# Score and value products that stream 32 copies of their one moving column, in a cached-attention decode kernel

## The chip, the cores and the metric

The kernel runs on one core of one Trainium2 chip. Its time is the device time in microseconds (us) of that core, the median of several runs. "Clock" is the share of its full clock that the throttle grants to TensorE; it is either 0.5 or 1.0 at any moment, so a mean is a share of time. In the trace of the kernel before it stays at one of them for whole multiples of 3.41 us (27 stretches, the last left out); a *window* is one such step of 3.41 us. A program on one core was fast in nearly all runs; the few slow are left out of ratios. The chip differed between the calls of the study, so runs are compared by way of the kernel before, which ran beside each of them.

## The reference, cut to what matters

One token, 32 heads, 32,768 cached keys of 128 numbers each, all bf16. K and V together are 537 MB, and each is read once.

```python
x = A_x
q = (_layernorm(x) @ wq)                        # 32 heads of 128
scores = einsum("bhqd,bhkd->bhqk", q, k_cache) * Dh ** -0.5
p = softmax(scores)
o = einsum("bhqk,bhkd->bhqd", p, v_cache)
h = x + o.reshape(1, 1, 4096) @ wo
h2 = h + B(_layernorm(h))                       # 512 -> 1376 -> 512, mish
```

## The kernel before

Keys lie on partitions. A *block* is 128 keys; a *group* is 8 blocks of one head (1,024 groups in all, 32 a head). For each group the PE transposes 8 blocks of K into PSUM, the DVE copies them to SBUF, and the PE multiplies each transposed block by the one column of q. Values lag by 42 groups: each block of V is multiplied by the one column of probabilities that belongs to it. K and V arrive through a ring of 160 KB a partition, in loads of 32 KB a partition (4.19 MB, 16 groups of K or of V). A load may start only when the PE has used up what lay in its place.

```python
def transposes(i):                   # group i
    ...
    for r in range(R):               # R = 8
        S.step(PE, lambda r=r: t_.matmul(
            tb[:, r * 128:(r + 1) * 128], block(ld, i, r), identb[:, :],
            is_transpose=True, start=True, stop=True), ...)

def scores(i):
    ...
    for r in range(R):
        c = (i % GH) * R + r
        S.step(PE, lambda r=r, c=c: t_.matmul(
            Sb[:, c:c + 1], kt[:, i % NE, r * 128:(r + 1) * 128], qT[:, h:h + 1], start=True, stop=True), ...)

def values(i):
    ...
    for r in range(R):
        c = (i % GH) * R + r
        S.step(PE, lambda r=r, c=c: t_.matmul(
            ob[:, 0:1], block(ld, i, r), pbuf[:, h % 2, c:c + 1],
            start=(c == 0), stop=(c == NCOL - 1)), ...)

for i in range(END):                 # order on the PE: transposes(i), scores(i - 2), values(i - 42)
    ...
    if 0 <= ho < H - 1 and (i - LAG) % GH == 3:
        y_cols(ho)                   # output projection of a finished head, as columns
    if i == NK + LAG + 8:            # near the end, once:
        for h in range(H - 1):
            y_mean(h)                # 62 matmuls
        for h in range(H - 1):
            y_row(h)                 # 124 matmuls, the same projection as rows
# after the loop: last head, layer norm, feed-forward, output
```

Of the kernel before, what the change touches and what calls it, by code (L numbers as in the profile page):

```python
# [19 lines left out]
RING_BYTES = 160 * 1024  # L20
LAG = 10
NSEM = 24


class _Sched:
# [89 lines left out]
def plan_loads(H, GH, ring_bytes, D, F):  # L115
# [26 lines left out]
    for i, ld in enumerate(loads):  # L142
# [11 lines left out]
        live = keep + [ld]  # L154
        if i >= NSEM:
            assert loads[i - NSEM].free is not None
            ld.after.append(loads[i - NSEM].free)
    return loads


def build_kernel(nc, A_x, A_k_cache, A_v_cache, A_wq, A_wo, B_w1, B_b1, B_w2, out, NE=3):
# [21 lines left out]
    def sb(shape, dt, name):  # L183
        cm = nc.sbuf_tensor(name, shape, dt)
        t = cm.__enter__()
        allocs.append(cm)
        return t.ap()
# [9 lines left out]
    kt = sb([128, NE, R * 128], BF16, "kt")  # L197
    pbuf = sb([128, 2, NCOL], BF16, "pbuf")
# [12 lines left out]
    qT = sb([128, 32], BF16, "qT")  # L211
# [40 lines left out]
    def view(ld):  # L252
        return ring[:, ld.off // 2:(ld.off + ld.nbytes) // 2]
# [6 lines left out]
    def block(ld, g, r):  # L260

        c = (g % GH) * R + r - ld.base
        return ring[:, ld.off // 2 + c * 128:ld.off // 2 + (c + 1) * 128]

    sem = nc.alloc_semaphore
    eng_sems = {PE: sem("ev_pe"), ACT: sem("ev_act"), DVE: sem("ev_dve"), POOL: sem("ev_pool"), SP: sem("ev_sp")}
    rsem = [sem(f"rsem{i}") for i in range(NSEM)]
    s_x = sem("s_x")
# [7 lines left out]
    def landed(ld):  # L276
        return (rsem[ld.idx % NSEM], 16 * (ld.idx // NSEM + 1))

    def program(S):
# [7 lines left out]
        def issue(ld):  # L287
            s = rsem[ld.idx % NSEM]
            dst = view(ld)
            if ld.kind in "kv":  # L290
                cache = A_k_cache if ld.kind == "k" else A_v_cache
                src = cache[0, ld.h, ld.base * 128:(ld.base + ld.n) * 128, :].rearrange("(m n) d -> m (n d)", m=128)
                S.dma(SP, lambda: sp.dma_start(dst, src).then_inc(s, 16), waits=ld.after)  # L293
            elif ld.kind == "wqa":
                S.dma(SP, lambda: sp.dma_start(
                    wqa, A_wq[:, 0:NH0 * Dh].rearrange("(p kc) n -> p kc n", kc=KC)).then_inc(s, 16), waits=ld.after)
            elif ld.kind == "wqb":
                S.dma(SP, lambda: sp.dma_start(
                    wqb, A_wq[:, NH0 * Dh:HD].rearrange("(p kc) n -> p kc n", kc=KC)).then_inc(s, 16), waits=ld.after)
            elif ld.kind == "w1":  # L300
                S.dma(SP, lambda: sp.dma_start(
                    w1v, B_w1.rearrange("(kc p) f -> p kc f", p=128)).then_inc(s, 16), waits=ld.after)
            else:
                S.dma(SP, lambda: sp.dma_start(
                    w2v[:, 0:FJ - 1, :],
                    B_w2[0:(FJ - 1) * 128, :].rearrange("(j p) n -> p j n", p=128)).then_inc(s, 16), waits=ld.after)
                S.dma(SP, lambda: sp.dma_start(
                    w2v[0:FLAST, FJ - 1, :], B_w2[(FJ - 1) * 128:F, :]).then_inc(s_w2, 16))
# [75 lines left out]
        def scores(i):  # L384
            h = i // GH
            Sb = S_b[h % 2]
            waits = [f"ev{i}", "qT0" if h < NH0 else "qT"]
            if i % GH == 0 and h >= 2:
                waits.append(f"exp{h - 2}")
            for r in range(R):  # L390
                c = (i % GH) * R + r
                S.step(PE, lambda r=r, c=c: t_.matmul(  # L392
                    Sb[:, c:c + 1], kt[:, i % NE, r * 128:(r + 1) * 128], qT[:, h:h + 1], start=True, stop=True),
                    name=(f"qkb{i}" if r == R - 1 else None), waits=(waits if r == 0 else ()))

        def values(i):
            h = i // GH
            ld = vload[i]
            ob = o_b[h % 2]
            waits = []  # L400
            if i % GH == 0:
                waits.append(f"exp{h}")
                if h >= 2:
                    waits.append(f"oT{h - 2}")
            if (i % GH) * R == ld.base:
                waits.append(landed(ld))
            for r in range(R):
                c = (i % GH) * R + r
                S.step(PE, lambda r=r, c=c: t_.matmul(  # L409
                    ob[:, 0:1], block(ld, i, r), pbuf[:, h % 2, c:c + 1],  # L410
                    start=(c == 0), stop=(c == NCOL - 1)),
                    name=(f"pv{i}" if r == R - 1 else None), waits=(waits if r == 0 else ()))

# [40 lines left out]
        for i in range(END):  # L454
# [11 lines left out]
            if 0 <= i - 2 < NK:  # L466
                scores(i - 2)
# [30 lines left out]
            if i - GH - LAG >= 0:  # L498
                values(i - GH - LAG)
# [41 lines left out]
        for j in range(FJ):  # L541
            W = 128 if j < FJ - 1 else FLAST
            for kc in range(KC):
                S.step(PE, lambda j=j, W=W, kc=kc: t_.matmul(  # L544
                    pre[0:W, j:j + 1], w1v[:, kc, j * 128:j * 128 + W], xcT[:, kc:kc + 1],
                    start=(kc == 0), stop=(kc == KC - 1)),
# [18 lines left out]
        for j in range(FJ):  # L565
            W = 128 if j < FJ - 1 else FLAST
            waits = ["act", landed(by_kind["w2"]), (s_w2, 16)] if j == 0 else ()
            for c in range(KC):
                S.step(PE, lambda j=j, W=W, c=c: t_.matmul(  # L569
                    yps[32 * c:32 * c + 1, HROW:HROW + 128], actT[0:W, j:j + 1], w2v[0:W, j, c * 128:(c + 1) * 128],  # L570
                    start=False, stop=(j == FJ - 1), skip_group_check=True),
# [47 lines left out]
```

## Time and profile before

| | before |
|---|---|
| time, median of 3 runs | 1389.87 us (1383.92 to 1392.62) |
| profiled span | 1381.0 us |
| PE busy | 96% |
| mean clock | 0.559 |
| DMA queue 1 (all loads), share of 16 engines | 95.0% |

These are lines of the page of the kernel before. Part 1 gives busy us, the share of the span and the count of instructions; part 2 cuts the span into 40 slices and gives tenths; part 3 gives packets, MB and share of the engines' time; part 4 is the chain of waits that ended last; part 5 gives busy us and mean ns of a group of instructions, then the idle time before it.

```profile
span 1381.0 us, 52251 instructions
PE 1326.2 (96%) x25319; PEld 1306.5 (95%) x25319; DVE 762.3 (55%) x1245; ACT 20.5 (1%) x70; POOL 2.5 (0%) x10
...
PE   6859999999999999999999999999999999999997
...
PEclk9856555555555565775565555555555555565556
DMA  9999999999999999999999999999999999999994
...
DMA packets 28298, 551.44 MB, mean 399 GB/s; under 512 B 2648, under 2 KB 8632, under 8 KB 11192
...
q1 hardware_dynamic: 27992, 548.09, 95.0%
q8 instruction: 198, 3.24, 0.9%
...
PE 94%; DMA 4%; issue 2%; SPq 0%; DVE 0%; ACT 0%
...
L373 PE MATMUL tps<-identb,ring 128*128 128x128 bf16 x8192 | 984.0, 296 | 19.5 <-DMA ring<-in_A_k_cache_dram 9.0
```

PE and DMA are both full, so the shares do not tell which one paces. The waits of the DMA's own queue (this view has: who waited for whom, us in total, times, the longest):

```profile
SPq L293 <- PE ops L409: 837.9, 61, 28.7
SPq L293 <- PE sps L392: 448.4, 61, 22.5
```

The queue waits for the PE to free the ring. The PE waits for loads only some 20 us in all:

```profile
PE ops L409 <- DMA ring<-in_A_v_cache_dram: 11.2, 1, 11.2
PE tps L373 <- DMA ring<-in_A_k_cache_dram: 9.0, 3, 4.8
```

The PE paces. The timeline (start, length, instruction) of the kernel before shows that it has two speeds, first at clock 0.5, then at clock 1.0:

```profile
660.64 1.01 PE L373 MATMUL tps<-identb,ring 128*128 128x128 bf16 x8
661.45 0.40 PE L392 MATMUL sps<-qT,kt 128*128 128x1 bf16 x8
661.71 0.35 PE L409 MATMUL ops<-pbuf,ring 128*128 128x1 bf16 x8
661.92 1.01 PE L373 MATMUL tps<-identb,ring 128*128 128x128 bf16 x8
...
700.72 0.61 PE L373 MATMUL tps<-identb,ring 128*128 128x128 bf16 x8
701.16 0.34 PE L392 MATMUL sps<-qT,kt 128*128 128x1 bf16 x8
701.37 0.34 PE L409 MATMUL ops<-pbuf,ring 128*128 128x1 bf16 x8
701.57 0.61 PE L373 MATMUL tps<-identb,ring 128*128 128x128 bf16 x8
```

Read starts, not lengths, for matmuls overlap. From transposes to the next transposes a group takes 1.28 us at half clock (660.64 to 661.92) and 0.85 us at full clock (700.72 to 701.57). K and V of a group need about 1.23 us of DMA: loads of 16 groups, of K or of V, land every 9.7 to 9.9 us in this trace when nothing holds them up. So the PE is a little slower than the DMA at half clock and far faster at full clock, and it runs at half clock most of the time.

### The profile page before, as it was taken

What the parts mean: (1) busy time and instruction counts of PE and PEld (TensorE: products, weight loads), DVE (VectorE), ACT (ScalarE), POOL (GpSimd) and SP (SyncE); (2) the same over time, 40 slices, a digit from 0 to 9 for tenths busy, and PEclk for the clock granted to TensorE, in tenths of its full rate; (3) what the DMA queues carried; (4) which work ended last, traced back from release to release, by engine and by line L of the source; (5) the groups of instructions that cost most, each with busy time, mean ns of one, the idle gap of its engine ahead of it and who ended that gap; (6) DMA issues with size and microseconds to landing.
All of it is one profiled execution on the core that took longest, in us unless ns stands there. A gap on an engine that the chain in (4) does not pass through costs nothing.

```text
span 1381.0 us, 52251 instructions
## 1 busy us (share of the span) xinstructions
PE 1326.2 (96%) x25319; PEld 1306.5 (95%) x25319; DVE 762.3 (55%) x1245; ACT 20.5 (1%) x70; POOL 2.5 (0%) x10
## 2 busy tenths in 40 slices
PE   6859999999999999999999999999999999999997
PEld 6859999999999999999999999999999999999997
DVE  5626555555555555665565555555555555555562
ACT  0000000000000000000000000000000000000000
POOL 0000000000000000000000000000000000000000
PEclk9856555555555565775565555555555555565556
DMA  9999999999999999999999999999999999999994
GB/s 390 402 422 419 433 425 430 428 396 414 402 385 417 390 396 411 420 421 421 419 410 417 409 387 397 403 391 404 395 391 407 392 393 396 385 428 387 389 391 156
DMA packets 28298, 551.44 MB, mean 399 GB/s; under 512 B 2648, under 2 KB 8632, under 8 KB 11192
## 3 DMA queue, kind: packets, MB, share of 16 engines
q1 hardware_dynamic: 27992, 548.09, 95.0%
q8 instruction: 198, 3.24, 0.9%
q14 instruction: 12, 0.10, 0.0%
q0 software_dynamic: 96, 0.00, 0.0%
HBM read 548.08 MB, written 0.00 MB: 397 GB/s over the span
## 4 chain that ended last, share of the span: by engine, by line
PE 94%; DMA 4%; issue 2%; SPq 0%; DVE 0%; ACT 0%
PE tps L373 60%; PE ops L409 16%; PE sps L392 14%; DMA ring<-in_A_k_cache_dram 4%; PE hlp L480 1%; PE hlp L485 1%; PE hlp L494 1%; SPq L293 0%; PE yps L431 0%; PE yps L417 0%; PE hlp L358 0%; PE yps L424 0%; PE sps L544 0%; PE yps L569 0%; DVE kt L382 0%
## 5 line engine op out<-in xcount | busy, mean ns | idle before, releaser
L382 DVE COPY kt<-tps 128x1024 bf16<-128x1024 bf16 x1024 | 707.2, 691 | 581.8 <-PE tps L373 580.7
L373 PE MATMUL tps<-identb,ring 128*128 128x128 bf16 x8192 | 984.0, 296 | 19.5 <-DMA ring<-in_A_k_cache_dram 9.0
L373 PEld LDWEIGHTS tps<-identb,ring 128*128 128x128 bf16 x8192 | 746.2, 134 | 23.7 <-issue 10.9
L392 PEld LDWEIGHTS sps<-qT,kt 128*128 128x128 bf16 x8192 | 412.2, 113 | 9.7 <-issue 9.5
L392 PE MATMUL sps<-qT,kt 128*128 128x1 bf16 x8192 | 401.1, 170 | 8.9 <-issue 8.8
L409 PE MATMUL ops<-pbuf,ring 128*128 128x1 bf16 x8192 | 355.6, 165 | 13.9 <-DMA ring<-in_A_v_cache_dram 11.2
L409 PEld LDWEIGHTS ops<-pbuf,ring 128*128 128x128 bf16 x8192 | 298.5, 104 | 26.4 <-issue 14.6
L489 ACT ACTIVATE pbuf<-sps,nbias 128x256 bf16<-128x256 f32 x32 | 15.1, 473 | 1334.4 <-DVE nbias L487 1334.4
L447 DVE TENSOR_REDUCE wbar<-wo_sb 128x1 f32<-128x512 bf16 x32 | 21.6, 674 | 0.0
L494 PE MATMUL hlp<-esum,onesm 128*128 128x1 f32 x64 | 17.9, 346 | 0.9 <-issue 0.9
L480 PE MATMUL hlp<-ident,pmax 128*1 128x128 f32 x64 | 18.4, 387 | 0.1
L485 PE MATMUL hlp<-gmax,onesr 1*128 1x1 f32 x64 | 18.1, 350 | 0.0
L494 PEld LDWEIGHTS hlp<-esum,onesm 128*128 128x128 f32 x64 | 15.8, 303 | 1.0 <-issue 1.0
L485 PEld LDWEIGHTS hlp<-gmax,onesr 1*128 1x128 f32 x64 | 15.4, 296 | 0.5
L476 DVE TENSOR_REDUCE pmax<-sps 128x1 f32<-128x256 f32 x32 | 13.3, 416 | 2.0 <-PE sps L392 2.0
L482 DVE TENSOR_REDUCE gmax<-hlp 1x1 f32<-1x128 f32 x32 | 8.9, 279 | 1.2 <-PE hlp L480 0.7
L417 PE MATMUL yps<-oT,wo_sb 128*128 128x1 bf16 x128 | 7.8, 165 | 0.3 <-DVE oT L530 0.3
L496 DVE RECIPROCAL rtotc<-hlp 128x1 f32<-128x1 f32 x32 | 5.4, 168 | 2.4 <-PE hlp L494 2.4
L358 PE MATMUL hlp<-xnT,ring 128*128 128x1 bf16 x128 | 3.8, 164 | 3.0 <-issue 3.0
L358 PEld LDWEIGHTS hlp<-xnT,ring 128*128 128x128 bf16 x128 | 3.6, 99 | 3.2 <-issue 3.1
L502 DVE TENSOR_SCALAR oT<-ops,rtotc 128x1 bf16<-128x1 f32 x31 | 6.6, 211 | 0.0
L530 DVE TENSOR_SCALAR oT<-ops,rtotc 128x1 bf16<-128x1 f32 x1 | 0.2, 221 | 11.2 <-PE ops L409 11.2
(69 smaller groups left out, 51.5 us busy)
## 6 DMA issues: line engine op xcount, KB each, us to landing
ring<-in_A_k_cache_dram SPq DMA_DIRECT2D x62, 4096.0 KB, 14.6
ring<-in_A_v_cache_dram SPq DMA_DIRECT2D x62, 4096.0 KB, 16.9
ring<-in_A_k_cache_dram SPq DMA_DIRECT2D x2, 2048.0 KB, 10.7
ring<-in_A_v_cache_dram SPq DMA_DIRECT2D x2, 2048.0 KB, 18.3
wo_sb<-in_A_wo_dram SPq DMA_DIRECT2D x1, 4096.0 KB, 37.7
ring<-in_A_wq_dram SPq DMA_DIRECT2D x1, 3584.0 KB, 30.2
ring<-in_A_k_cache_dram SPq DMA_DIRECT2D x2, 1024.0 KB, 9.6
ring<-in_A_v_cache_dram SPq DMA_DIRECT2D x2, 1024.0 KB, 22.4
```

The costliest lines, as they stand in the source:

```text
L373: S.step(PE, lambda r=r: t_.matmul(tb[:, r * 128:(r + 1) * 128], block(ld, i, r), identb[:, :], is_transpose=True, start=True, stop=True), ...
L382: S.step(DVE, lambda: v.tensor_copy(kt[:, i % NE, :], T_b[i % 2][:, :]), name=f"ev{i}", waits=waits)
L392: S.step(PE, lambda r=r, c=c: t_.matmul(Sb[:, c:c + 1], kt[:, i % NE, r * 128:(r + 1) * 128], qT[:, h:h + 1], start=True, stop=True), name ...
L409: S.step(PE, lambda r=r, c=c: t_.matmul(ob[:, 0:1], block(ld, i, r), pbuf[:, h % 2, c:c + 1], start=(c == 0), stop=(c == NCOL - 1)), name= ...
L417: S.step(PE, lambda c=c: t_.matmul(yps[:, c:c + 1], wo_sb[:, h, c * 128:(c + 1) * 128], oT[:, h:h + 1], start=False, stop=(h == H - 1), sk ...
L447: S.step(DVE, lambda: v.tensor_reduce(wbar[:, h:h + 1], wo_sb[:, h, :], AXX, ALU.add), waits=[(s_wo, 16)], name=f"wbar{h}")
L476: S.step(DVE, lambda hp=hp: v.tensor_reduce(pmax[:, hp:hp + 1], S_b[hp % 2][:, 0:NCOL], AXX, ALU.max), name=f"pmax{hp}", waits=[f"qkb{hp * ...
L480: S.step(PE, lambda hp=hp: t_.matmul(A_REG, pmax[:, hp:hp + 1], ident[:, :], start=True, stop=True), name=f"A{hp}", waits=[f"pmax{hp}", "i ...
L482: S.step(DVE, lambda hp=hp: v.tensor_reduce(gmax[0:1, hp:hp + 1], A_REG, AXX, ALU.max), name=f"gmax{hp}", waits=[f"A{hp}"])
L485: S.step(PE, lambda hp=hp: t_.matmul(B_REG, onesr[0:1, :], gmax[0:1, hp:hp + 1], start=True, stop=True), name=f"B{hp}", waits=[f"gmax{hp}" ...
L489: S.step(ACT, lambda hp=hp: a.activation(pbuf[:, hp % 2, :], S_b[hp % 2][:, 0:NCOL], ACTF.Exp, bias=nb[:, hp:hp + 1], scale=SC, accum_out= ...
L494: S.step(PE, lambda hp=hp: t_.matmul(C_REG, onesm[:, :], esum[:, hp:hp + 1], start=True, stop=True), name=f"C{hp}", waits=[f"exp{hp}"])
```

## The change

The intent: each product with a one-column moving operand streams 32 copies of it, so that the array is seen to be busier and the throttle grants the full clock. The extra result columns are overwritten or never read. There are no more instructions than before, and their order is the same.

```diff
+WIDE = 32
@@ scores
-                    Sb[:, c:c + 1], kt[:, i % NE, r * 128:(r + 1) * 128], qT[:, h:h + 1], start=True, stop=True),
+                    Sb[:, c:c + WIDE], kt[:, i % NE, r * 128:(r + 1) * 128], qT[:, h:h + 1].to_broadcast([128, WIDE]),
+                    start=True, stop=True),
@@ values
-                    ob[:, 0:1], block(ld, i, r), pbuf[:, h % 2, c:c + 1],
+                    ob[:, 0:WIDE], block(ld, i, r), pbuf[:, h % 2, c:c + 1].to_broadcast([128, WIDE]),
                     start=(c == 0), stop=(c == NCOL - 1)),
```

## The prediction

> **What bounds it now.** The page shows PE busy 96% of a 1381 us span, DMA queue 1 busy 95%, mean granted clock 0.559. The chain of waits is 94% PE, 4% DMA. The queue's own waits are nearly all for PE lines (838 + 448 us): loads wait until PE frees ring space. PE paces the kernel, the DMA close behind.
>
> Per group of 8 blocks (1024 groups) the timeline shows two speeds: 1.28 us at clock 0.5 (transposes 107 ns start to start, scores and values 27 ns), 0.85 us at clock 1.0 (55 and 25 ns). A full-size load (4.19 MB) lands every 9.7 to 9.9 us when not held up (87 to 247 us), about 426 GB/s, so K and V of a group need 1.23 us.
>
> **Why the clock is low.** Granted stretches last multiples of 3.41 us[...]. In the slow steady state the array streams 8x128 + 16 = 1040 columns in 1.28 us, 68%[...]. The clock rises only after windows in which most transposes fall (22 to 24, about 75%), and falls after starved ones. I infer that streamed columns are counted, transposes included, with a threshold near 75%.[...]
>
> **The change** removes nothing, moves no instruction, and adds 31 streamed columns to each of 16,384 products. Cost at half clock: 32 columns are 26.7 ns by estimate (128 take 107), within the 27 ns[...]. At full clock 14 ns, under the 25 ns spacing. So about +0. Benefit: activity at half clock goes to 1536 columns[...], so every busy half-clock window should lift the clock.
>
> **Then DMA binds.** PE needs at most about 16 us for 16 groups, even with two half-clock windows (6.8 us, 5.3 groups, the rest at 0.85), against 19.8 us of DMA. PE will starve some us every 16 groups and the clock will drop then: mixed, but off the critical path. Estimate: 128 full loads x 9.9 = 1268 us, output weights 13, other weights about 16, start 2.5: DMA ends near 1300. PE, now 14 us behind when the last V lands (1358 to 1372), should be under 1 us behind. The last V lands 3.5 us before the last weights; from the last value product to the end stays 8.6 us. Span 1306 to 1310, plus 2 us outside it.
>
> **Predicted: 1312 us, 8 in 10 within 1296 to 1340. Faster by over 2%: 0.92; within 2%: 0.05; slower: 0.03.**
>
> **What would show it.** Mean clock 0.7 to 0.85; products still 27 and 25 ns apart; a chain mostly DMA; queue 1 busy 98% or more, about 420 GB/s; PE waits on K and V loads of 200 us or more; PE busy near 75%.
>
> **What would make it wrong.** If 32 columns don't overlap the weight load (54 ns, or slow reads of a repeated element), half clock costs 1.7 us a group: possibly slower. If the clock counts something else, it stays near 0.55 and nothing changes. If DMA can't hold 426 GB/s while PE runs fast, 1330 to 1345. Long clock drops shrink the gain.

128 full loads 1268 us, output weights 13, other weights 16 and the start 2.5 make 1299.5, the "near 1300" of the text. All four are from the trace before: 13 is what the landing of the output weights adds to one interval between loads (22.9 us in place of 9.7), 16 is an estimate (7.0 MB at 426 GB/s), 2.5 us is when the first input lands. The 68% is a share of the 1536 columns that transposes one after the other, 128 columns every 106.7 ns on average in that trace, would stream in 1.28 us. The estimates of 26.7 and 14 ns for 32 columns are a quarter of the 107 and 55 ns of a transpose, and 54 ns is 27 measured plus 26.7 estimated; that wider products would cost nothing was not shown before the result.

## The result, and the profile after

| | before | after |
|---|---|---|
| time, median of the fast runs of this comparison (4 each) | 1388.09 us | 1332.03 us |
| ratio, 95% interval | | 0.9595 (0.9558 to 0.9632) |
| profiled span | 1381.0 us | 1331.3 us |
| PE busy | 96% | 77% |
| mean clock | 0.559 | 0.889 |
| last V lands / last value product done | 1358.1 / 1372.4 us | 1314.4 / 1322.6 us |

A ratio is the mean time of one kernel's fast runs over that of the other's of the same rounds, so it is not quite the ratio of the medians. The change is faster by 4%. The lines of the page after that answer to those above:

```profile
span 1331.3 us, 52251 instructions
PE 1031.1 (77%) x25319; PEld 999.0 (75%) x25319; DVE 753.8 (57%) x1245; ACT 20.5 (2%) x70; POOL 2.5 (0%) x10
...
PE   6838778777788778877778778778778777777776
...
PEclk9879888889888898898899889899888898898885
DMA  9999999999999999999999999999999999999993
...
DMA packets 28298, 551.44 MB, mean 414 GB/s; under 512 B 2648, under 2 KB 8632, under 8 KB 11192
...
q1 hardware_dynamic: 27992, 548.09, 97.4%
q8 instruction: 198, 3.24, 1.0%
...
DMA 66%; PE 31%; issue 2%; SPq 0%; DVE 0%; ACT 0%
...
L375 PE MATMUL tps<-identb,ring 128*128 128x128 bf16 x8192 | 701.6, 234 | 171.7 <-DMA ring<-in_A_k_cache_dram 133.5
```

The chain has turned from PE to DMA, and the PE has gaps in every slice. Instruction for instruction nothing got slower: products start 27 to 28 ns apart at half clock and 25 ns at full clock, as before. The waits of the PE in the kernel after:

```profile
PE tps L375 <- DMA ring<-in_A_k_cache_dram: 133.5, 58, 5.6
PE sps L394 <- issue: 48.0, 35, 2.3
PE ops L412 <- issue: 46.5, 36, 2.4
PE tps L375 <- issue: 35.7, 33, 2.3
PE ops L412 <- DMA ring<-in_A_v_cache_dram: 16.5, 3, 15.0
```

Two kinds of idle time share the gaps: 150 us for loads and 130 us of "issue", in which nothing that the profile shows is waited for. The second kind comes 104 times, 1.25 us on average, and is new in this size (20 us in the kernel before). It is a wait for instructions. Queue q8 brings them in packets of 16 KB, one every 6.5 us or so, and all 96 "issue" waits of the PE over 0.5 us end 1.2 to 1.6 us after such a packet has ended. In the kernel before the same holds for all 16 of them.

Landing times, read from the loads' semaphores, give the pace of the DMA. Over 110 loads in the middle of the trace a load lands every 10.02 us on average after, against 10.37 us before. But the pace is not even: most intervals are 9.7 us, and 21 of the 110 are about 11.3 us, one in five or six. Finally the tail of the kernel after, from its timeline (brackets: idle time of the engine before it):

```profile
1307.72 1.26 PE L427 MATMUL yps<-oT,wbh 128*128 128x1 bf16 x42
1310.95 0.69 PE L427 MATMUL yps<-oT,wbh 128*128 128x1 bf16 x20 [1.97 <-issue]
1311.57 3.05 PE L434 MATMUL yps<-wo_sb,oT 128*1 128x128 bf16 x108
1317.16 0.59 PE L434 MATMUL yps<-wo_sb,oT 128*1 128x128 bf16 x16 [2.54 <-issue]
1317.68 4.94 PE L412 MATMUL ops<-pbuf,ring 128*128 128x32 bf16 x184
1322.66 0.22 DVE L533 TENSOR_SCALAR oT<-ops,rtotc 128x1 bf16<-128x1 f32 x1 [15.54 <-PE ops L412]
```

The last V lands at 1314.4 us. The PE is then still in the block of means and rows, in which it waits twice for instructions; 184 value products come after it.

### The profile page after: what moved, and what is told of

Its sections match the earlier page's. It is cut to its first block, busy times and chain, and to the rows that moved or that the text cites. A ratio compares the mean times of both kernels' runs of the same rounds, so it can differ in the third digit from the quotient of the medians.

```text
span 1331.3 us, 52251 instructions
## 1 busy us (share of the span) xinstructions
PE 1031.1 (77%) x25319; PEld 999.0 (75%) x25319; DVE 753.8 (57%) x1245; ACT 20.5 (2%) x70; POOL 2.5 (0%) x10
## 4 chain that ended last, share of the span: by engine, by line
DMA 66%; PE 31%; issue 2%; SPq 0%; DVE 0%; ACT 0%
DMA ring<-in_A_k_cache_dram 64%; PE tps L375 16%; PE ops L412 7%; PE sps L394 6%; DMA ring<-in_A_v_cache_dram 2%; PE hlp L483 1%; PE hlp L488 1%; PE hlp L497 1%; PE yps L434 0%; SPq L295 0%; PE yps L427 0%; PE sps L547 0%; PE yps L572 0%; SPq L297 0%; PE yps L420 0%
## 5 line engine op out<-in xcount | busy, mean ns | idle before, releaser
L375 PE MATMUL tps<-identb,ring 128*128 128x128 bf16 x8192 | 701.6, 234 | 171.7 <-DMA ring<-in_A_k_cache_dram 133.5
L375 PEld LDWEIGHTS tps<-identb,ring 128*128 128x128 bf16 x8192 | 523.6, 104 | 183.2 <-DMA ring<-in_A_k_cache_dram 137.3
L394 PE MATMUL sps<-qT,kt 128*128 128x32 bf16 x8192 | 382.6, 180 | 48.2 <-issue 48.0
L412 PE MATMUL ops<-pbuf,ring 128*128 128x32 bf16 x8192 | 366.1, 179 | 63.1 <-issue 46.5
L394 PEld LDWEIGHTS sps<-qT,kt 128*128 128x128 bf16 x8192 | 334.6, 100 | 51.2 <-issue 51.1
L412 PEld LDWEIGHTS ops<-pbuf,ring 128*128 128x128 bf16 x8192 | 283.9, 98 | 77.0 <-issue 59.6
L497 PE MATMUL hlp<-esum,onesm 128*128 128x1 f32 x64 | 12.0, 253 | 1.0 <-issue 0.9
L488 PE MATMUL hlp<-gmax,onesr 1*128 1x1 f32 x64 | 12.3, 259 | 0.0
L497 PEld LDWEIGHTS hlp<-esum,onesm 128*128 128x128 f32 x64 | 9.8, 192 | 1.0 <-issue 1.0
L492 ACT ACTIVATION_READ_ACCUMULATOR pbuf<-sps,nbias 128x1 f32 x32 | 6.2, 193 | 0.0
```

Of the source, the lines that this page charges most:

```text
L375: S.step(PE, lambda r=r: t_.matmul(tb[:, r * 128:(r + 1) * 128], block(ld, i, r), identb[:, :], is_transpose=True, start=True, stop=True), ...
L394: S.step(PE, lambda r=r, c=c: t_.matmul(Sb[:, c:c + WIDE], kt[:, i % NE, r * 128:(r + 1) * 128], qT[:, h:h + 1].to_broadcast([128, WIDE]), ...
L412: S.step(PE, lambda r=r, c=c: t_.matmul(ob[:, 0:WIDE], block(ld, i, r), pbuf[:, h % 2, c:c + 1].to_broadcast([128, WIDE]), start=(c == 0), ...
L488: S.step(PE, lambda hp=hp: t_.matmul(B_REG, onesr[0:1, :], gmax[0:1, hp:hp + 1], start=True, stop=True), name=f"B{hp}", waits=[f"gmax{hp}" ...
L492: S.step(ACT, lambda hp=hp: a.activation(pbuf[:, hp % 2, :], S_b[hp % 2][:, 0:NCOL], ACTF.Exp, bias=nb[:, hp:hp + 1], scale=SC, accum_out= ...
L497: S.step(PE, lambda hp=hp: t_.matmul(C_REG, onesm[:, :], esum[:, hp:hp + 1], start=True, stop=True), name=f"C{hp}", waits=[f"exp{hp}"])
```

## The experiments

Theory: the throttle counts streamed columns, transposes among them; the change lifts that count over a threshold, the PE is no longer the pace, and the DMA binds. Rivals: transposes do not count; the gain grows with the columns themselves; the PE still co-limits through its stalls. A second question came with the result: where do the 11.3 us intervals come from?

A caution for all that follows. The comparison with the reference passed even for a run that leaves out seven of eight products of most heads. Attention adds too little to this output for that comparison to see it. So "correct" says little about attention here, for any kernel in this document.

### The phase run: what the clock counts

Edit: the whole program is replaced by PE phases over one loaded block of K, with an idle stretch before each (wrong result). The core of it:

```diff
+PHASES = [("N", 1), ("T", 0), ("N", 8), ("M", 1), ("N", 16), ("M", 4), ("N", 20),
+          ("M", 8), ("N", 24), ("M", 16), ("N", 28), ("M", 32), ("N", 32)]
+# T: transposes; N: products with n columns; M: 8 transposes, 16 products with n columns
+# before each phase the PE waits for two large memsets on the DVE
```

> A kernel of PE phases alone (wrong result on purpose, no ring, no loads but one of 256 KB): each phase of some 50 us at half clock is preceded by an idle stretch on PE, so each starts at half clock. Phases in order: products with 1 column; transposes; products with 8 columns; the group mix (8 transposes, 16 products) with 1 column; products 16; mix 4; products 20; mix 8; products 24; mix 16; products 28; mix 32; products 32. My theory (the clock counts streamed columns, transposes included, with a threshold near 75%): clock stays 0.5 in products 1, 8, 16, 20 (3 to 62%[...]); rises within two windows (6.8 us) in transposes (100%), products 28 and 32, mix 16 and 32 (83%, 100%); products 24 and mix 1, 4, 8 (75%, 68, 71, 75%) lie near the threshold: mix 1 late or not at all, mix 8 soon. Rival (transposes do not count, only ordinary products do): the transposes phase stays at 0.5 to its end, and mix 16 or 32 (17%, 33%) rises only if products 8 (25%) rises too.

Measured, with each phase's activity (columns streamed, as a share of those that transposes one after the other stream in the same time at half clock, 128 every 107 ns), and when the clock rose after the phase's start:

| phase | activity | clock rose after | then |
|---|---|---|---|
| products, 1 / 8 / 16 / 20 columns | 3 / 25 / 49 / 62% | never in 50 us | |
| mix, 1 column (the kernel before) | 68% | never in 51 us | |
| mix, 4 columns | 71% | 11.2 us | stayed |
| mix, 8 columns | 75% | 7.4 us | stayed |
| products, 24 columns | 74% | 4.6 us | fell again after 10.2 us |
| mix, 16 columns | 83% | 4.9 us | stayed |
| products, 28 columns | 86% | 6.4 us | fell once after 24 us, back 3.4 us later |
| mix, 32 / products, 32 columns | 100 / 99% | 2.6 / 5.0 us | stayed |
| transposes alone | 100% | 4.6 us | stayed |

Lines of the view by windows of that run (columns: window, its length and the PE's busy us; then busy us of the other engines, granted clock, DMA share, GB/s), for the mix with 1 column, the mix with 4, and the transposes:

```profile
270.80:322.00 51.20, 51.20 (x960) 51.20 (x960) 0.00 (x0) 0.00 (x0) 0.50 0.01 3
442.50:480.20 37.70, 37.70 (x958) 37.70 (x959) 0.00 (x0) 0.00 (x0) 0.85 0.01 3
121.40:150.30 28.90, 28.90 (x479) 28.90 (x480) 0.00 (x0) 0.00 (x0) 1.00 0.01 2
```

PE busy is 100% in all three, so it is not busy time that is counted. Columns fit: with the transposes counted in full, the mix stayed at half clock at a mean of 68% and rose at 71%, so the threshold of this run lies between the two. The rival falls. The kernel before sits just under it, which is why its clock rose only now and then. My guess of 75% was for single windows of 3.41 us, and is not settled: those that ended in a rise hold 75% or more here and 71% or more in the kernel before, but other windows of up to 76% brought no rise.

The way down is another count. At full clock transposes start 55 to 56 ns apart in place of 107, so shares are here taken of twice as many columns. In this run every window that ended in a fall held at most 36% of them, and every one that did not, 39% or more; in the kernel before these figures are 35 and 36%, and in the other traces the two kinds overlap between 34 and 39%. Products with 24 columns stayed up through two windows at 40%; they fell, and those with 28 too, in a window with a gap of 0.5 or 0.8 us in which the PE waited for instructions.

### Few bytes, one column and 32: the PE without the DMA

Edit, on top of either kernel (wrong result). A first try of both, cut from head 2 on and to one eighth, was REFUSED before the chip, because a part of the ring was read unwritten; it gave no result. This is the second:

```diff
+                if ld.h >= 4:
+                    cut = ld.nbytes // 16
+                    dst, src = dst[:, 0:cut], src[:, 0:cut]
```

> The refused one-column kernel again, with the K and V loads of heads 4 to 31 cut to one sixteenth (wrong result on purpose; the ring is written in full before, so nothing is read unwritten). PE alone sets the pace from head 4 on. If starved windows were what kept the kernel before at half clock: the clock rises early and stays, mean above 0.85, span about 1020 to 1090 us. If 68% activity is too little by itself (the phase run left the same mix at half clock for its whole 51 us): clock stays near 0.5 with few stretches of 1.0 at per-head work, span 1300 to 1380 us. In that kernel no starved window ends a stretch of 1.0, so such stretches should be long.

> The same cut (heads 4 to 31, one sixteenth of the bytes) in the changed kernel, 32 columns. PE is the only limit at 0.85 us a group: about 150 us for the first four heads at the pace of DMA, 900 groups x 0.85 = 765, extras 40 and the tail: 960 to 1030 us, mean clock above 0.95. Instruction stalls of PE should nearly vanish[...]: under 40 us against 130 us in the changed kernel. Rival (PE co-limits the changed kernel): over 1200 us.

Measured, one run each: one column 1072.86 us, clock 0.834; 32 columns 1002.85 us, clock 0.968, with instruction waits on the PE of about 19 us in place of 130. With most of the DMA's work gone the changed kernel runs in 1003 us. The cut removes most of the PE's instruction waits too, but with their 130 us added it would still be far under 1332. So the DMA, not the PE, holds it there, and that rival falls.

The one-column run is the more instructive. Its clock fell to 0.5 at 76 us, stayed there for 307 us (the first 90 or so still under full loads), rose at 383 us and then stayed at 1.0 for 662 us, to the tail. So two things held the kernel before at half clock. At 68% it seldom crosses the threshold (I had said early; it took 307 us). And each rise is short, but not for want of loads: in the kernel before, the PE waits for its last load at 97 us. Each of its nine falls between 100 and 1360 us ends a window of 3.41 us in which the PE waited 0.4 to 1.9 us for instructions. This wait comes before the fall at 708.6 us:

```profile
707.26 0.25 PE L392 MATMUL sps<-qT,kt 128*128 128x1 bf16 x4 [1.61 <-issue]
```

At full clock the PE uses its instructions up 1.5 times as fast (0.85 us a group in place of 1.28), and under full loads their packets then come too late. In the few-bytes run such waits add up to 6 us. Once up and fed, one column is enough: 1040 columns in 0.85 us are 51% by the count at full clock.

### Widths 4 and 8

Edit: `WIDE = 4`, and `WIDE = 8`.

> WIDE = 4 in place of 32: activity at half clock 70.8% (1088 of 1536). The phase run lifted the clock of this mix after 11 us and kept it. Theory of a threshold near 70%: after each starved stretch about 11 us at half clock (8.7 groups), then fast: 16 groups in about 17.4 us, still under the DMA's 19.9, so mean clock 0.65 to 0.85 and 1332 to 1352 us. If per-head work and phase leave it under the threshold: clock under 0.6 and over 1370 us, as before. If the gain grew with the columns themselves (31 extra give 56 us, 3 give a tenth): about 1380 us.

> WIDE = 8: activity 75% at half clock. The phase run lifted the clock of this mix after 7.4 us. Threshold theory: at most three half-clock windows after a starved stretch, 16 groups in about 16.5 us, DMA paces: clock 0.75 to 0.88, 1331 to 1341 us. If the gain were proportional to the extra columns (7 of 31 of 56 us): about 1375 us.

| WIDE | mean clock (profiled run) | median | ratio to before of the same rounds |
|---|---|---|---|
| 4 | 0.638 | 1351.88 us (1337.67 to 1357.28) | 0.9713 (0.9616 to 0.981) |
| 8 | 0.784 | 1332.59 us (1331.57 to 1334.71) | 0.9591 (0.9562 to 0.962) |
| 32 | 0.889 | 1332.03 us | 0.9595 (0.9558 to 0.9632) |

Eight columns give all of the gain, at a lower mean clock, and four give some 70% of it by the mean ratios, though the interval for four is wide (2 to 4% faster). It is a threshold, not a proportion, by which four would have given a tenth. Above it, more clock buys nothing (1332.59 us at 0.784, 1332.03 at 0.889), because the DMA binds. The 4-column run varied by 20 us, and its clock (just under my range) and time lie at the edge. Of its 30 falls between 70 and 1300 us, 29 come with an instruction wait, and after a fall it can rise late (the longest stretch at half clock is 154 us).

### Products cut: the DMA's floor, and the periodic step

Edit, on the changed kernel (wrong result), for transposes, scores and values alike; the start flag of the values follows:

```diff
-            for r in range(R):
+            for r in (range(R) if i < 2 * GH else [R - 1]):
```

> The changed kernel with all its loads, but from head 2 on only one transpose, score and value product of each eight (wrong result on purpose): the DMA floor, and about 7 of 8 PE instructions gone, so few instruction blocks to fetch. Theory A (the periodic extra 1.5 us in every fifth to sixth load, 11.3 against 9.7 us, is PE's instruction blocks taking DMA time): loads land every 9.7 us nearly throughout, last V about 30 us earlier, span 1285 to 1302 us. Theory B (the periodic step belongs to the loads or the memory): the step stays at one in five or six loads, span 1318 to 1330 us. Either way at most 8 us of the changed kernel's tail goes with PE's backlog.

Measured: 1294.65 us (4 runs within 0.4 us), ratio 0.9351. Intervals are 9.7 us nearly throughout: only 4 of 110 exceed 10.5 us. Its instruction queue:

```profile
q8 instruction: 40, 0.66, 0.2%
```

There are 40 packets of 16 KB against 198. The last V lands at 1284.1 us, 30.3 us earlier than in the changed kernel, and 8.9 us later all is done, against 16.9. This is what theory A said, but the run also took away the PE's reads of the ring, so it does not tell A from B alone.

### Instructions put back without their work

Edit, on the run with products cut: where an instruction was dropped, a 1 x 1 matmul stands in its place.

```diff
+                if r < R - 1 and i >= 2 * GH:
+                    S.step(PE, lambda: t_.matmul(
+                        Sb[0:1, 400:401], oneb[0:1, 0:1], oneb[0:1, 0:1], start=True, stop=True), ...)
+                    continue
```

> The run with products cut (1294.65 us), but each of the seven transposes, scores and values taken out of eight is replaced by a 1 x 1 matmul with its own weight load: the instruction count is that of the changed kernel again, the array's work and its reads of the ring stay small. Theory A (instruction blocks cost the DMA about 0.19 us each): the step of 1.5 us in every fifth to sixth load is back, instruction queue near 198 packets, last V near 1314 us, span 1322 to 1334 us. Theory B (it was PE's reads of the ring, or its fast work, that disturbed the loads): loads stay at 9.7 us, span 1290 to 1300 us.

> As the run with 1 x 1 matmuls in place, but only the cut scores and values are replaced, the cut transposes are left out: PE[...] should no longer pace anything, and the instruction blocks are two thirds of the way back (about 145 packets against 40 and 198). Theory A (0.19 us of DMA per block, from 30.3 us over 158 blocks): last V at 1284 + 105 x 0.19 = 1304 us, 1311 to 1322 us in all. Theory B (PE's reads of the ring and fast work disturb the loads): last V at 1284 to 1288 us, under 1303 us in all.

The first of them, with all three kinds put back, was a poor experiment. It took 1347.94 us: small as they are, these matmuls cost the PE so much that a group took 1.2 us, the PE was 97% busy and paced again. The longer intervals were back and the last V landed at 1316.7 us, but with two limits so close it proves little.

The second, with scores and values alone put back, left the PE 74% busy at half clock:

| run | instruction packets | last V lands | intervals over 10.5 us, of 110 |
|---|---|---|---|
| products cut | 40 | 1284.1 us | 4 |
| two thirds put back | 145 | 1302.1 us | 15 |
| the changed kernel | 198 | 1314.4 us | 21 |

It took 1319.25 us, with the last V within 2 us of theory A's figure and 14 us beyond theory B's range, though these matmuls read nothing of the ring and the clock was 0.526. So the step is the PE's instruction stream on the DMA engines: 30.3 us over 158 packets is 0.19 us each, and by that estimate about 38 us of the changed kernel's time. In the trace of the changed kernel a 16 KB instruction packet takes 0.9 to 1.1 us, and nine in ten of them overlap with exactly one 32 KB load packet that takes about 1.7 us in place of 1.22. How the longer packet becomes the longer interval is not shown.

### The tail moved into the loop

Edit, on the changed kernel. The sums of the output weights are also spread over the first part of the loop, so that the means have them in time.

```diff
                 y_cols(ho)
+                y_row(ho)
...
-            if i == NK + LAG + 8:
-                for h in range(H - 1):
-                    y_mean(h)
-                for h in range(H - 1):
-                    y_row(h)
+            if i > WB + 4 and ym_next < H - 1 and (ym_next < ho or (ym_next == ho and (i - LAG) % GH > 3)):
+                y_mean(ym_next)
+                ym_next += 1
```

> The changed kernel itself, on the chip of this call, so that the next two can be compared with it: 1328 to 1335 us.

> The changed kernel with the output rows and means of heads 0 to 30 moved out of the tail: the rows right after the head's output columns, the means one a step from the middle on (the sums of the output weights are taken earlier for it). Nothing added, nothing removed. In the changed kernel 10 us of the last 22 lie in that block (5.5 us of matmuls, 4.5 us waiting for instructions), and the last V lands 8 us before PE reaches it. Expected: PE finishes within 1 us of the last V, 5 to 8 us saved, about 1324 us, and the last V lands where it did. Rival (the waits for instructions move to other places of the tail, or the second weights land last): under 3 us saved.

Measured in the same rounds, 6 runs each: the changed kernel 1331.60 us (ratio 0.9604), this one 1324.62 us (0.9551; 1323.94 to 1325.64). The 7.0 us are inside what was expected. The last V lands at 1313.6 us as it did (1313.5), and the PE finishes 1.6 us later, in place of 8.2 in the first profile of the changed kernel and 5.5 in that of these rounds; I had said within 1 us.

### Packed value products

Edit, on the last one: p is the stationary operand and four blocks of V the moving one; the four diagonal blocks of the result are added once a head.

```diff
+                for r in range(0, R, 4):
+                    c = (i % GH) * R + r
+                    o = ld.off // 2 + (c - ld.base) * 128
+                    S.step(PE, lambda r=r, c=c, o=o: t_.matmul(
+                        ob[0:4, 0:512], pbuf[:, h % 2, c:c + 4], ring[:, o:o + 512],
+                        start=(c == 0), stop=(c == NCOL - 4)), ...)
```

> The last one, and value products packed: four columns of the weights are the stationary operand and four blocks of V (512 columns) the moving one, two matmuls a group in place of eight; the diagonal 128-column blocks of the 4 x 512 result are added by four small matmuls a head (last head as before). PE instructions fall by a quarter, from 198 blocks to about 150. Theory A: 48 x 0.19 = 9 us of DMA back, 1311 to 1319 us; clock above 0.9, since half of the array's time more is streaming. PE needs about 1.07 us a group, so its margin to the DMA (1.23) is thin: if instruction stalls of 0.1 us a group come on top, PE paces again and it takes 1320 to 1345 us.

It failed: 1379.56 us (ratio 0.9943), with clock 0.986 and 152 packets. Both figures were as hoped, but the PE paced, at 1.27 us a group (the 1.07 was an estimate: 8 transposes at 55 ns, 8 scores at 25 and 1024 columns of V at 55 for 128):

```profile
700.56 0.09 PEld L416 LDWEIGHTS ops<-ring,pbuf 128*4 128x4 bf16 x2
700.56 0.59 PE L416 MATMUL ops<-ring,pbuf 128*4 128x512 bf16 x2
701.08 0.45 PEld L377 LDWEIGHTS tps<-identb,ring 128*128 128x128 bf16 x8 [0.44 <-issue]
701.09 0.62 PE L377 MATMUL tps<-identb,ring 128*128 128x128 bf16 x8
```

The two matmuls need 0.43 us (215 ns each, as measured in the next run), but the next transposes start 0.53 us after the first of them, and their weight load does not start before. In all, 107 ns pass before the packed matmuls in place of 25, and 311 ns after the second in place of 215. The weight load does not run beside the streaming here: PEld is idle for 0.44 us before it. The next edit asks whether the narrow stationary operand is the reason:

```diff
-                        ob[0:4, 0:512], pbuf[:, h % 2, c:c + 4], ring[:, o:o + 512],
+                        ob[:, 0:512], pbuf[:, h % 2, c:c + 128], ring[:, o:o + 512],
```

(p is padded with zeros; rows from 4 on of the result are not used.)

> The packed value products once more. In the last run PE needed 1.27 us a group at full clock in place of 1.07: after the matmuls with a 4-column stationary operand the next transposes started 311 ns later in place of 215, and before them 107 ns passed in place of 25. Here the stationary operand is 128 columns of the weights (only the first four rows of the result are used), so that it loads like every other and its load can hide. Expected: those gaps at 215 and 25 ns, PE 1.07 us a group, no pacing by PE, 152 blocks, last V near 1306 us, 1312 to 1322 us in all against 1324.6 with the tail moved alone. Rival (the drain belongs to the 512-column matmul itself): 1.27 us a group again, about 1380 us. Between: instruction stalls make PE pace, 1322 to 1345 us.

Measured: 1314.80 us (1314.41 to 1315.21), ratio 0.9462 (0.944 to 0.9484). The same place of its timeline:

```profile
701.32 0.12 PEld L418 LDWEIGHTS ops<-ring,pbuf 128*128 128x128 bf16 x2
701.35 0.59 PE L418 MATMUL ops<-ring,pbuf 128*128 128x512 bf16 x2
701.56 0.65 PEld L378 LDWEIGHTS tps<-identb,ring 128*128 128x128 bf16 x8
701.77 0.61 PE L378 MATMUL tps<-identb,ring 128*128 128x128 bf16 x8
```

The load of the transposes' weights now starts 0.21 us before them, the gaps are 215 and 25 ns, and a group takes 1.08 us. The last V lands at 1303.5 us, 10 us earlier than with 198 packets, which repeats the cost of an instruction packet (10 us over 46 packets, 0.22 us each) in a kernel that does its full work. This version beats both kernels: 1.4% under the changed one, by the ratios 0.9462 and 0.9595, each against the kernel before in its own rounds. That its attention is exact is not shown, by the caution above.

## Why the prediction was right, and what of it was off

The prediction was right: 1332.03 us lies in its range, and the change is faster, as forecast. The point, 1312 us, was 20 us too low.

- **Why the clock was low, and that it would rise: right.** The phase run shows that columns count and that transposes do. In the mean the threshold lies between 68 and 71% (phase run), and for single windows my 75% is not settled; at 100% the difference does no harm. I had put the falls down to "starved" windows in an aside. They were half of the story, and in the kernel before they come with waits for instructions, not for loads. In the kernel after, of 58 falls between 70 and 1300 us, 29 come with load waits, 24 with instruction waits and 5 with both.
- **No cost of the columns: right.** Products start 27 to 28 and 25 ns apart, as predicted.
- **DMA binds afterwards: right.** The chain is 66% DMA and a PE freed of the DMA needs 1003 us. PE busy 77% was foreseen (near 75%); the clock, 0.889, came out above my 0.7 to 0.85.
- **The failed step, first term: "128 full loads x 9.9 = 1268 us ... DMA ends near 1300".** It ended at 1318. The middle of the trace ran at 10.02 us a load, so this term is about 15 us more. I had averaged a stretch of 16 intervals with three long ones in it, took the long ones for chance, and did not ask what they were. They are PE's instruction packets, a cost that the change leaves as it was. The prediction had allowed for a DMA that can't hold 426 GB/s, with 1330 to 1345 us, and this is where the time fell (4.19 MB in 10.02 us are 419 GB/s), but it looked for the reason in a fast PE.
- **The failed step, second term: "PE, now 14 us behind when the last V lands ..., should be under 1 us behind".** It was 8.2 us behind (5.5 in a later profile of the same kernel). I had read 5.5 us of means and rows in the tail of the kernel before, but not that they would stand between the PE and the last V, and that instruction waits of 2.0 and 2.5 us would come on top. Moving them away gave 7.0 us.
- **PE waits on loads "of 200 us or more": wrong.** They were 150 us; another 130 us went to instruction waits, which fall to about 19 us when the DMA is nearly idle. So they go with loaded DMA queues, and with the PE's pace: the full-width packed kernel, which takes 1.08 us a group, had 3 us of them under full loads.
- The last term, 8.6 us from the last value product to the end, was exact. With a last V at 1296.5, 1 us and 8.6 us I had 1306 us of span; 1314.4, 8.2 and 8.6 make 1331.

What stays open: which count of columns in a single window lifts the clock, why the instruction packets come late, and how one of them delays a whole load.

## What to carry to other kernels

Here matmuls of one column and of 32 start the same 27 to 28 ns apart at half clock and 25 ns at full clock, so the extra columns were free, and they bought most of the full clock (mean 0.559 to 0.889). Look for such a spacing, and find the smallest width that lifts the clock (8 columns gave 0.784 and all of the gain), for past the point where another engine binds, more clock buys nothing. Look also for what takes the clock down again: in the kernel after it was about as often a wait for instructions as one for data (24 and 29 of 58 falls). When a change hands the pace to the DMA, size the DMA's floor by an experiment that takes the compute away, since the average over a stretch hides periodic costs such as the compute engine's own instruction stream (0.19 us a packet here, 38 us in all by estimate). After that, fewer instructions and a shorter tail can be worth more than a faster engine (1314.80 us here against 1332), and a narrow stationary operand may cost more than it saves (1379.56 us with 4 columns, 1314.80 with 128).
